# Scaling two units per group inside the FFN products, casting v a group later, and adding part of the product sums on VectorE

## The chip, the cores and the metric

The kernel runs on one core of a Trainium2 chip. A core has TensorE (PE) for matmuls, VectorE (DVE), ScalarE (ACT) and GpSimd (POOL) for elementwise work, and SyncE (SP), which here issues nearly all transfers between memory and the core. Each engine works through its own queue in order; an instruction that must wait holds everything behind it on that queue. The metric is the device time of one execution in microseconds (us), as the median of several runs.

## The reference

Linear attention with a decay per head, and then a feed-forward network (FFN) with a product of two linear maps:

```
for b in range(nb):                       # blocks of the sequence, with a running state
    intra = (qb @ kb.T) * Dmask           # Dmask[i, j] = lam ** (i - j) for i >= j
    out[:, :, sl] = intra @ vb + (qb * lam_pow) @ kv_state
    kv_state = lam_block * kv_state + (kb * rev_pow).T @ vb
...
a = x @ w_a                               # x: the attention's output, 3072 x 512
b = x @ w_b                               # w_a, w_b: 512 x 1536
return (a * b) @ w_out                    # w_out: 1536 x 512
```

q, k and v have 4 batches, 8 heads, 768 positions and 64 dimensions in f32; the result is 3072 x 512 in f32.

## The kernel before

The 3072 rows are cut into 24 *units* of 128 positions, six to a batch. The units are worked on in eight groups of 4, 1, 2, 4, 4, 4, 4 and 1 units (`GROUPS`). While the FFN of group g runs, the attention of the next group's units is prepared in its gaps. So units 0 to 3 are group 0, unit 4 is group 1, 5 and 6 are group 2, 7 to 10 group 3, 11 to 14 group 4, 15 to 18 group 5, 19 to 22 group 6 and 23 group 7.

The order of all work is written out by hand: the program's order is the order on each engine. An FFN calls `hook(slot)` at numbered slots, and the table `PLAN` says, for each group, which piece of work goes at which slot:

- `PK` (`prep_k`): q and k of a unit are multiplied by powers of the decay and become bf16 (two `scale` instructions on POOL, line 283, tile `qk`); then SP issues a transposing DMA of the result (line 313, tile `qkT`).
- `PV` (`prep_v`): v of a unit is cast to bf16 (line 300, on ACT from unit 9 on; tile `vb`), and `pump` is called. `P` is `PK` and `PV` together.
- `S`: the scores of a unit (`kq`, line 341, PE) and their masks (`m`, line 358, DVE).
- `V` (`piece_V`): the unit's part of the state, added into the PSUM bank `kvd` (line 405, PE), and a masked copy of that bank (`st`, line 438, DVE). The last unit of a batch (5, 11, 17, 23) has nothing to do here.
- `Q` and `O2` (`pieces_O`): the attention output of two units (`o_ps`, line 375), its cast into the FFN's input `xT` (line 398, ACT), the state's part of the second unit (line 427) and its copy (line 438). `Q` also makes the scores and masks of the two units that follow.
- `TW` (`w_sums`): sums and differences of weight pieces for the FFN with seven products (tile `tw`, line 515, DVE).
- `W`: one of the seven output rows held back in SBUF from the early groups is stored.

`pump` issues loads in the order of the list `pending`. A load of q, k or v of unit c goes out when c is less than `used` plus two (three up to unit 8), where `used` is the number of units already scaled. All loads, the transposes and the stores of finished rows share SP's queue.

Groups 3 to 6 use `ffn_seven`: the two linear maps are worked out with seven block products instead of eight, for six pairs of column blocks i. A product is four matmuls of 256 columns into a PSUM bank (`m_q`, `m_r`, `m_p`, line 544). Between the products, ACT copies banks to SBUF (line 559: `s1`, `s5`, `s2`, `u2`) and DVE adds (lines 586, `c12`; 592, `c22`; 595, the product with `m_q`). Product 2 goes into `m_p`; ACT copies it, and POOL adds it to the copy of product 1:

```
                snap("s2", p, 0, d["s12"][:, 1])
                bank["held"].discard(pb)
                d["c11"] = a_pool.tile([128, 2, 256], BF16, name="c11", tag="a")
                nc.gpsimd.tensor_add(d["c11"], d["s12"][:, 0], d["s12"][:, 1])
```

POOL then multiplies `c11` and `c12` into the FFN's inner tile `ab` (line 588). The products follow each other in this order, one per step s, for all i: `((0, 1), (2, 5), (3, 2), (4, 6), (6, 3), (8, 7), (12, 4))` gives offset from 7i and number of the product. Slot 2j lies at s = 7j + 1 and slot 2j + 1 at s = 7j + 4, up to slot 10. Slot 11 follows the last step but one. Then come the output matmuls (`op`, line 647), six at a time: slots 12 to 19 lie between these half rows, and a finished row of 128 x 512 is copied by ACT (`o_sb`, line 642) and stored by SP (line 643).

Of the kernel before, what the change touches and what calls it, by code (L numbers as in the profile page):

```python
# [17 lines left out]
BF16 = mybir.dt.bfloat16  # L18
# [4 lines left out]
def _bc(ap, dims):  # L23
# [7 lines left out]
W_HALVES = (4, 5)  # L31
W_BUFS = 11
LOOKAHEAD = {9: 2, 10: 1}
DMA_T = range(7, 24)
KEEP_GROUPS = 3
PACK = 4
# [4 lines left out]


S_GROUPS = (3, 4, 5, 6)
PLAN = {
# [11 lines left out]
}  # L56
for _g, _u in ((3, 11), (4, 15), (5, 19)):
    PLAN.setdefault(_g, []).extend(
        [(11, "PK", _u + 4), (11, "V", _u), (12, "PK", _u + 5), (12, "PV", _u + 4), (13, "Q", (_u, _u + 1, _u + 2, _u + 3)),
         (15, "V", _u + 2), (17, "O2", (_u + 2, _u + 3)), (18, "S", _u + 4)])  # L60
    if _u + 5 > 23:
        PLAN[_g].remove((12, "PK", 24))
    else:
        PLAN[_g] += [(14, "PV", _u + 5), (16, "P", _u + 6), (18, "P", _u + 7), (19, "S", _u + 5)]
PLAN[3] += [(1, "PK", 13), (3, "PK", 14), (8, "PV", 13), (11, "PV", 14)]
PLAN[3] += [(_s, "W", None) for _s in (9, 9, 9, 10, 10, 10, 10)]
PLAN[0] += [(7, "TW", (0, "dve")), (7, "TW", (1, "dve")), ]
PLAN[2] += [(_s, "TW", (4 + _n // 4, "dve", (_n % 4,)))
            for _n, _s in enumerate((2, 3, 5, 6, 8, 15, 15, 15))]


@with_exitstack
def kernel(
# [11 lines left out]
    nc = tc.nc  # L85
    B, H, S, D = q.shape
# [5 lines left out]
    NU = B * NB  # L92
# [12 lines left out]
    a_pool = ctx.enter_context(tc.tile_pool(name="a", bufs=5))  # L105
# [28 lines left out]
    def load_x(w, u):  # L134
        b, nb = divmod(u, NB)
        t = ld_pool.tile([128, H, D], F32, name=w + "f", tag=w + "f", bufs=4 if w == "v" else 3)
        nc.sync.dma_start(out=t, in_={"q": qr, "k": kr, "v": vr}[w][b, nb])  # L137
        raw[u, w] = t
# [16 lines left out]
    def load_w(kind, c):  # L155
        t = wst_pool.tile([128, 1024], F32, name="wst", tag="wst")
        if kind == "o":
            t = t[:].rearrange("p (k n) -> p k n", k=2)
            nc.sync.dma_start(out=t, in_=wo_r[:, 2 * c:2 * c + 2, :])
        else:  # L160
            w = W_CHUNKS[c]
            t = t[:, :KS * w].rearrange("p (k n) -> p k n", k=KS)
            r = wa_r if kind == "a" else wb_r
            if c in W_HALVES:
                t = t.rearrange("p k n -> p (k n)").rearrange("p (k n) -> p k n", k=2)
            nc.sync.dma_start(out=t, in_=w_part(r, c))
        staged[kind, c] = t
# [17 lines left out]
    pending = []  # L185
# [3 lines left out]
    pending += [("o", c) for c in range(4)] + [("q", n0), ("k", n0)]  # L189
    pending += [("o", 4), ("o", 5), ("v", n0)]  # L190
    for u in range(n0 + 1, NU):
        pending += [("q", u), ("k", u), ("v", u)]
    used = {"u": 0}

    def pump():
        while pending:
            kind, c = pending[0]
            if kind in "abo":
                if len(staged) >= W_BUFS:
                    return  # L200
            elif c >= used["u"] + LOOKAHEAD.get(used["u"], 2 if used["u"] > 8 else 3):
                return
            pending.pop(0)
            if kind in "abo":
                load_w(kind, c)
            else:
                load_x(kind, c)
# [26 lines left out]
    for u in range(n0):  # L234
        load_x("v", u)
    pump()


# [66 lines left out]
    def prep_k(u):  # L305
        make_ks(u, "dve" if u < n0 + 2 else "pool")
        make_qs(u, "pool")
        used["u"] = u + 1
        if u in (13, 14):
            pump()  # L310
        if u in DMA_T:
            qkT = qkT_pool.tile([128, 2, HP, 128], BF16, name="qkT", tag="qkT")
            nc.sync.dma_start_transpose(  # L313
                out=qkT[:].rearrange("p j hp i -> p (j hp) i"),
                in_=U[u]["qk"][:].rearrange("p j h d -> p (j h d)"))
            U[u]["qT"], U[u]["kT"] = qkT[:, 0], qkT[:, 1]

    def prep_v(u):
        make_vb(u, "pool" if u < n0 + 3 else "dve" if u < n0 + 5 else "act")
# [197 lines left out]
    def sums(u):  # L517
        g = next(i for i in range(len(GROUPS)) if g_u0[i] <= u < g_u0[i] + GROUPS[i])
        if g not in S_GROUPS or u != g_u0[g] + 3:
            return  # L520
# [11 lines left out]
    def ffn_seven(g, u0, xT, hook):  # L532
# [23 lines left out]
        def snap(name, ps, bufs, t=None):  # L556
            if t is None:
                t = sn_pool.tile([128, 2, 256], F32, name=name, tag=name, bufs=bufs)
            nc.scalar.copy(t, ps)  # L559
            return t  # L560

        def step(i, n):
            d = live.setdefault(i, {})
            if n == 1:
                d["q"], d["qb"] = bank_of("m_q")
                product(i, d["q"], w_of(wa_sb, 0, i), x11, True)
                d["s12"] = wst_pool.tile([128, 2, 2, 256], F32, name="s12", tag="wst")
                snap("s1", d["q"], 0, d["s12"][:, 0])
            elif n == 5:
                d["r"], d["rb"] = bank_of("m_r")  # L570
                product(i, d["r"], t_of(0, i), st[:, 0], True)
                d["s5"] = snap("s5", d["r"], 2)
            elif n == 2:
                p, pb = bank_of("m_p")
                product(i, p, w_of(wa_sb, 2, i), x12, True)
                snap("s2", p, 0, d["s12"][:, 1])
                bank["held"].discard(pb)
                d["c11"] = a_pool.tile([128, 2, 256], BF16, name="c11", tag="a")
                nc.gpsimd.tensor_add(d["c11"], d["s12"][:, 0], d["s12"][:, 1])  # L579
            elif n == 6:  # L580
                product(i, d["q"], t_of(1, i), st[:, 1], False)
                d["u2"] = snap("u2", d["q"], 1)
            elif n == 3:
                product(i, d["r"], w_of(wb_sb, 2, i), st[:, 3], False)
                c12 = sn_pool.tile([128, 2, 256], F32, name="c12", tag="c12", bufs=2)
                nc.vector.tensor_add(c12, d["u2"], d["r"])  # L586
                bank["held"].discard(d["rb"])
                nc.gpsimd.tensor_mul(ab[:, 2 * i:2 * i + 2, 0:256], d["c11"], c12)  # L588
            elif n == 7:
                product(i, d["q"], t_of(2, i), st[:, 2], False)  # L590
                d["c22"] = sn_pool.tile([128, 2, 256], F32, name="c22", tag="c22", bufs=1)
                nc.vector.tensor_add(d["c22"], d["s5"], d["q"])
            else:
                product(i, d["q"], t_of(3, i), x22, False)
                nc.vector.tensor_mul(ab[:, 2 * i:2 * i + 2, 256:512], d["c22"], d["q"])  # L595
                bank["held"].discard(d["qb"])
                live.pop(i)
# [239 lines left out]
    for g, n in enumerate(GROUPS):  # L837
# [33 lines left out]

        if g in S_GROUPS:
            ffn_seven(g, g_u0[g], gx.pop(g), hook)
# [31 lines left out]
```

## Time and profile before

| | before |
|---|---|
| median of 3 runs | 233.31 us (233.29 to 234.09) |
| the profiled execution's time | 231.28 us |
| its span, first to last instruction | 229.6 us |
| mean granted clock of TensorE | 0.993 |
| busy: PE, DVE, ACT, POOL | 217.9, 143.6, 120.8, 110.4 us |
| bytes moved | 39.40 MB |

The profiled execution is one single execution; its rows give start and duration in us from the start of the span. On a row of a timeline, the brackets at the end tell how long the engine had stood idle just before, and which instruction ended that idle time. A row may stand for several like instructions (x4); its duration is then that of all of them. Matmuls overlap, so that of two rows the difference of their starts is the pace, not the duration shown. In a row of windows stand the stretch, its length, the busy time of PE, weight loads, DVE, ACT and POOL, the granted clock as a share of full speed, the share of the DMA engines and the GB/s.

### The profile page before, as it was taken

The numbers are of one execution on the slowest core, as the hardware profiler recorded it, in microseconds if no ns is written. First come the engines' busy times: TensorE is split into PE (matmuls) and PEld (weight loads), VectorE is DVE, ScalarE is ACT, GpSimd is POOL, SyncE is SP. The second block draws the span as 40 slices with busy tenths as digits, with TensorE's granted clock in tenths as the row PEclk, the third lists the DMA queues.
The fourth block names the chain that finished last, engine by engine and source line by source line (L and its number), as shares of the span: only waits on it lengthen the run. The fifth ranks groups of instructions, "written<-read, shape, count | busy, mean of one in ns | idle before, by whom it ended". The sixth has DMA issues, their size and how long they took to land.

```text
span 229.6 us, 5404 instructions
## 1 busy us (share of the span) xinstructions
PE 217.9 (95%) x2127; PEld 149.6 (65%) x2127; DVE 143.6 (63%) x252; ACT 120.8 (53%) x237; POOL 110.4 (48%) x115
## 2 busy tenths in 40 slices
PE   7799999999999997999989999968999999999994
PEld 2475444459688576885548885436886558885494
DVE  0994888986489597669175667039665645663050
ACT  3686564056555565773347663147664337771251
POOL 6061000237455469998338778064878006773000
PEclk9999999999999999999999999997999999999999
DMA  4999999999999999996999902999200421001211
GB/s 134 314 259 353 361 387 302 292 219 198 214 215 171 221 194 222 179 303 203 223 234 234 177 3 49 157 254 251 72 0 3 109 79 46 1 3 46 87 52 46
DMA packets 97544, 39.40 MB, mean 172 GB/s; under 512 B 85488, under 2 KB 92016, under 8 KB 97520
## 3 DMA queue, kind: packets, MB, share of 16 engines
q1 hardware_dynamic: 97232, 39.00, 75.8%
q8 instruction: 16, 0.26, 0.5%
q10 hardware_dynamic: 288, 0.07, 0.1%
q14 instruction: 8, 0.07, 0.1%
HBM read 28.32 MB, written 6.29 MB: 151 GB/s over the span
## 4 chain that ended last, share of the span: by engine, by line
PE 71%; DMA 13%; SPq 5%; DVE 4%; ACT 2%; POOL 2%; issue 1%; ACTq 0%; POOLq 0%
PE op L647 19%; PE m_q L544 17%; PE b_ps L478 9%; PE m_r L544 8%; PE a_ps L478 8%; PE m_p L544 5%; DMA vf<-in_v_dram 4%; DMA out_dram<-o_sb 4%; DMA wst<-in_moe_w_b_dram 3%; SPq L137 3%; PE o_ps L375 3%; DMA q<-in_q_dram 2%; PE kq L341 2%; POOL qk L283 2%; SPq L313 1%
## 5 line engine op out<-in xcount | busy, mean ns | idle before, releaser
L647 PE MATMUL op<-wo_sb,ab 128*128 128x512 bf16 (+2 forms) x312 | 67.3, 363 | 0.0
L647 PEld LDWEIGHTS <-ab 128*128 128x128 bf16 x312 | 28.0, 98 | 27.3
L544 PEld LDWEIGHTS <-tw 128*128 128x128 bf16 x384 | 37.7, 98 | 8.6 <-issue 2.3
L579 POOL TENSOR_TENSOR c<-s 128x512 bf16<-128x512 f32 x24 | 30.6, 1274 | 21.9 <-ACT s L559 21.8
L283 POOL TENSOR_TENSOR qk<-kf,lp_k 128x512 bf16<-128x512 f32 x18 | 19.0, 1054 | 28.8 <-DMA kf<-in_k_dram 25.9
L283 POOL TENSOR_TENSOR qk<-qf,lp_q 128x512 bf16<-128x512 f32 x20 | 21.8, 1091 | 22.7 <-DMA qf<-in_q_dram 22.7
L505 DVE TENSOR_TENSOR ab<-a_sb,b_ps 128x128 bf16<-128x128 bf16 (+2 forms) x48 | 19.3, 417 | 21.4 <-ACT a_sb L487 18.5
L588 POOL TENSOR_TENSOR ab<-c,c 128x512 bf16<-128x512 bf16 x24 | 28.0, 1165 | 6.6 <-DVE c L586 6.2
L595 DVE TENSOR_TENSOR ab<-c,m_q 128x512 bf16<-128x512 f32 x24 | 16.5, 688 | 22.0 <-PE m_q L544 22.0
L358 DVE TENSOR_TENSOR m<-kq,lotri 128x512 bf16<-128x512 f32 x45 | 28.0, 682 | 2.0 <-PE kq L341 1.9
L544 PE MATMUL m_q<-xs,tw 128*128 128x256 bf16 x192 | 29.2, 275 | 0.0
L478 PE MATMUL b_ps<-xT,wb_sb 128*128 128x128 bf16 (+2 forms) x192 | 27.7, 272 | 0.3 <-DVE wb_sb L182 0.3
L478 PE MATMUL a_ps<-xT,wa_sb 128*128 128x128 bf16 (+2 forms) x200 | 27.7, 268 | 0.1
L642 ACT COPY o_sb<-op 128x512 f32<-128x512 f32 (+2 forms) x19 | 10.3, 541 | 31.9 <-PE op L647 29.2
L544 PEld LDWEIGHTS <-wa_sb 128*128 128x128 bf16 x192 | 18.9, 99 | 5.9 <-issue 2.9
L487 ACT CAST a_sb<-a_ps 128x128 bf16<-128x128 f32 (+2 forms) x48 | 17.1, 376 | 10.4 <-PE a_ps L478 9.5
L559 ACT COPY s<-m_q 128x512 f32<-128x512 f32 x24 | 14.1, 587 | 12.5 <-PE m_q L544 11.6
L478 PEld LDWEIGHTS <-wa_sb 128*128 128x128 bf16 x200 | 16.1, 98 | 6.6 <-DVE wa_sb L182 0.3
L478 PEld LDWEIGHTS <-wb_sb 128*128 128x128 bf16 x192 | 15.7, 98 | 6.5 <-DVE wb_sb L182 0.8
L586 DVE TENSOR_TENSOR c<-u,m_r 128x512 f32<-128x512 f32 x24 | 16.3, 680 | 3.2 <-ACT u L559 3.2
L544 PE MATMUL m_p<-xT,wa_sb 128*128 128x256 bf16 x96 | 14.8, 278 | 2.5 <-ACT o_sb L642 2.5
L300 ACT CAST vb<-vf 128x512 bf16<-128x512 f32 x15 | 9.3, 627 | 14.7 <-DMA vf<-in_v_dram 13.6
(85 smaller groups left out, 301.3 us busy)
## 6 DMA issues: line engine op xcount, KB each, us to landing
vf<-in_v_dram SPq DMA_DIRECT2D x24, 256.0 KB, 4.8
qf<-in_q_dram SPq DMA_DIRECT2D x20, 256.0 KB, 4.5
kf<-in_k_dram SPq DMA_DIRECT2D x20, 256.0 KB, 4.8
out_dram<-o_sb SPq DMA_DIRECT2D x16, 256.0 KB, 3.4
wst<-in_moe_w_a_dram SPq DMA_DIRECT2D x6, 512.0 KB, 8.4
wst<-in_moe_w_b_dram SPq DMA_DIRECT2D x6, 512.0 KB, 8.8
wst<-in_moe_w_out_dram SPq DMA_DIRECT2D x6, 512.0 KB, 10.6
out_dram<-o_kept SPq DMA_DIRECT2D x7, 256.0 KB, 3.7
```

Source lines behind the costliest of these rows:

```text
L283: eng_of(eng).tensor_mul(dst.rearrange("p (c b) d -> p b c d", b=2), x[:].rearrange("p (b c) d -> p b c d", b=2), lp.rearrange("p (b c) o ...
L358: nc.vector.tensor_mul(m, kq[i], lotri_bc)
L478: nc.tensor.matmul(ps[:, lo:hi], lhsT=w_sb[:, s, f * 128:(f + 1) * 128], rhs=xT[:, s, lo:hi], start=(s == 0), stop=(s == KS - 1), skip_gro ...
L487: nc.scalar.copy(a_sb[:, :gt], ps[:, :gt])
L505: nc.vector.tensor_mul(ab[:, f, :gt], a_sb[:, :gt], ps[:, :gt])
L544: nc.tensor.matmul(ps[:, f, :], lhsT=w(k, f), rhs=x[:, k, :], start=(first and f == 0 and k == 0), stop=True, skip_group_check=True)
L559: nc.scalar.copy(t, ps)
L579: nc.gpsimd.tensor_add(d["c11"], d["s12"][:, 0], d["s12"][:, 1])
L586: nc.vector.tensor_add(c12, d["u2"], d["r"])
L588: nc.gpsimd.tensor_mul(ab[:, 2 * i:2 * i + 2, 0:256], d["c11"], c12)
L595: nc.vector.tensor_mul(ab[:, 2 * i:2 * i + 2, 256:512], d["c22"], d["q"])
L647: nc.tensor.matmul(op[:, lo:hi], lhsT=ab[:, f, t * 128:(t + 1) * 128], rhs=wo_sb[:, f, lo:hi], start=(f == 0), stop=(f == FC - 1))
```

## The change

- From unit 15 on (`V_LATE`), v is put two units later in the list of loads, and goes out only once its own unit has been scaled; `prep_k` calls `pump` behind the transpose for these units.
- `PK` of unit 15 moves from slot 11 to slot 7 of group 3; 16, 17 and 18 go to slots 12, 14 and 17. In group 4, `PK` of 19 and 20 moves to slots 6 and 9, among the products, 21 and 22 to slots 13 and 16; `PK` of 23 to slot 6 of group 5. Before, four units of a group were scaled at slots 11, 12, 16 and 18.
- `PV` of units 15 to 18 moves from the end of group 3 to slots 1, 3, 5 and 8 of group 4, `PV` of 19 to 22 likewise to group 5, and of 23 to slot 1 of group 6.
- In groups 3, 4 and 5, `V` of the third unit moves from slot 15 to 14, and the second `O2` from slot 17 to 16.
- For the i listed in `SUM_ON_VEC`, DVE adds product 2 straight from PSUM into `c11`; ACT's copy `s2` and POOL's addition are left out. These are 4, 3, 3 and 4 of the six i in groups 3, 4, 5 and 6.
- The last eight pieces of weight sums, before at slots 2, 3, 5, 6, 8 and three times 15 of group 2, go to slots 10, 10 and 12 of group 1 and 2, 3, 5, 6 and 12 of group 2.

```diff
+V_LATE = 15
+SUM_ON_VEC = {3: (1, 2, 3, 4), 4: (2, 3, 4), 5: (2, 3, 4), 6: (1, 2, 3, 4)}
...
-    3: [(11, "S", 11), (11, "S", 12)],
-    6: [(13, "O", 23)],
+    3: [(1, "PK", 13), (3, "PK", 14), (8, "PV", 13), (11, "PV", 14), (11, "S", 11), (11, "S", 12),
+        (7, "PK", 15), (12, "PK", 16), (14, "PK", 17), (17, "PK", 18)],
+    4: [(6, "PK", 19), (9, "PK", 20), (13, "PK", 21), (16, "PK", 22)],
+    5: [(6, "PK", 23)],
+    6: [(1, "PV", 23), (13, "O", 23)],
 }
 for _g, _u in ((3, 11), (4, 15), (5, 19)):
-    PLAN.setdefault(_g, []).extend(
-        [(11, "PK", _u + 4), (11, "V", _u), (12, "PK", _u + 5), (12, "PV", _u + 4), (13, "Q", (_u, _u + 1, _u + 2, _u + 3)),
-         (15, "V", _u + 2), (17, "O2", (_u + 2, _u + 3)), (18, "S", _u + 4)])
-    if _u + 5 > 23:
-        PLAN[_g].remove((12, "PK", 24))
-    else:
-        PLAN[_g] += [(14, "PV", _u + 5), (16, "P", _u + 6), (18, "P", _u + 7), (19, "S", _u + 5)]
-PLAN[3] += [(1, "PK", 13), (3, "PK", 14), (8, "PV", 13), (11, "PV", 14)]
+    PLAN[_g] += [(11, "V", _u), (13, "Q", (_u, _u + 1, _u + 2, _u + 3)), (14, "V", _u + 2),
+                 (16, "O2", (_u + 2, _u + 3)), (18, "S", _u + 4)]
+    if _g < 5:
+        PLAN[_g] += [(19, "S", _u + 5)]
+    if _g > 3:
+        PLAN[_g] += [(1, "PV", _u), (3, "PV", _u + 1), (5, "PV", _u + 2), (8, "PV", _u + 3)]
...
+PLAN[1] += [(10, "TW", (4, "dve", (0,))), (10, "TW", (4, "dve", (1,))), (12, "TW", (4, "dve", (2,)))]
 PLAN[2] += [(_s, "TW", (4 + _n // 4, "dve", (_n % 4,)))
-            for _n, _s in enumerate((2, 3, 5, 6, 8, 15, 15, 15))]
+            for _n, _s in enumerate((2, 3, 5, 6, 12), 3)]
...
-        pending += [("q", u), ("k", u), ("v", u)]
+        pending += [("q", u), ("k", u)]
+        if u < V_LATE:
+            pending += [("v", u)]
+        elif u >= V_LATE + 2:
+            pending += [("v", u - 2)]
+    pending += [("v", NU - 2), ("v", NU - 1)]
...
+            elif kind == "v" and c >= V_LATE:
+                if c >= used["u"]:
+                    return
...
+        late = u >= V_LATE
         if u in DMA_T:
...
+        if late:
+            pump()
...
-                snap("s2", p, 0, d["s12"][:, 1])
+                d["c11"] = a_pool.tile([128, 2, 256], BF16, name="c11", tag="a")
+                if i in SUM_ON_VEC[g]:
+                    nc.vector.tensor_add(d["c11"], d["s12"][:, 0], p)
+                else:
+                    snap("s2", p, 0, d["s12"][:, 1])
+                    nc.gpsimd.tensor_add(d["c11"], d["s12"][:, 0], d["s12"][:, 1])
                 bank["held"].discard(pb)
-                d["c11"] = a_pool.tile([128, 2, 256], BF16, name="c11", tag="a")
-                nc.gpsimd.tensor_add(d["c11"], d["s12"][:, 0], d["s12"][:, 1])
```

## The prediction

> **What bounds the kernel now.** I read four things in this order: the busy shares and the chain on the profile's page, TensorE's timeline for its idle pieces, the timelines of the engines that those pieces name, and the windows for the granted clock.
>
> ```profile
> PE 217.9 (95%) x2127; PEld 149.6 (65%) x2127; DVE 143.6 (63%) x252; ACT 120.8 (53%) x237; POOL 110.4 (48%) x115
> ...
> PE   7799999999999997999989999968999999999994
> ...
> PE 71%; DMA 13%; SPq 5%; DVE 4%; ACT 2%; POOL 2%; issue 1%; ACTq 0%; POOLq 0%
> ```
>
> TensorE (PE) is busy 95% of a span of 229.6 us and carries 71% of the chain; no other engine passes 63%. So only time in which TensorE stands still, or runs slowly, can be won. The 40 slices of 5.74 us show three weak spots inside the run: slice 15 (a 7), slice 20 (an 8) and slices 26 and 27 (6 and 8). They are the starts of groups 3, 4 and 5. TensorE's timeline gives their idle pieces, and two windows the clock:
>
> ```profile
> 88.56 0.60 PE L544 MATMUL m_q<-xT,tw 128*128 128x256 bf16 x4 [1.61 <-DVE c L592]
> ...
> 119.52 0.60 PE L544 MATMUL m_p<-xT,wa_sb 128*128 128x256 bf16 x4 [0.94 <-ACT o_sb L642]
> ...
> 152.17 0.38 PE L341 MATMUL kq<-qkT 64*128 64x128 bf16 x7 [0.75 <-ACT o_sb L642]
> ...
> 153.61 0.60 PE L544 MATMUL m_r<-xs,tw 128*128 128x256 bf16 x4 [0.35 <-DVE xs L524]
> 155.80 1.01 PE L544 MATMUL m_p<-xT,wa_sb 128*128 128x256 bf16 x4 [1.59 <-ACT o_sb L642]
> ...
> 158.80 0.60 PE L544 MATMUL m_q<-xs,tw 128*128 128x256 bf16 x4
> ...
> 152.60:155.80 3.20, 1.20 (x9) 0.77 (x9) 2.63 (x3) 1.76 (x5) 2.23 (x2) 0.87 1.20 294
> 155.80:158.80 3.00, 3.00 (x17) 2.16 (x16) 3.00 (x7) 2.09 (x4) 1.26 (x1) 0.56 1.26 231
> ```
>
> Idle at the three starts: 1.61; 0.94; 0.75 + 0.35 + 1.59 = 2.69 us; together 5.24 us. Besides, the granted clock (the column after the five engines) falls to 0.56 behind the last of them: from 155.80 to 158.80 only four products run, 3.00 us. In the steady state a product takes 0.437 us (below), four of them 1.75, so the slow clock costs 1.25 us.
>
> Why ScalarE (ACT) is late at the starts of groups 4 and 5:
>
> ```profile
> 118.15 0.62 ACT L300 CAST vb<-vf 128x512 bf16<-128x512 f32 x1 [2.77 <-DMA vf<-in_v_dram]
> ...
> 151.02 0.62 ACT L300 CAST vb<-vf 128x512 bf16<-128x512 f32 x1 [5.88 <-DMA vf<-in_v_dram]
> ...
> 154.43 0.62 ACT L300 CAST vb<-vf 128x512 bf16<-128x512 f32 x1 [1.33 <-DMA vf<-in_v_dram]
> 155.16 0.59 ACT L642 COPY o_sb<-op 128x512 f32<-128x512 f32 x1
> ...
> 188.99 0.59 ACT L642 COPY o_sb<-op 128x512 f32<-128x512 f32 x1 [2.45 <-issue]
> 189.61 0.60 PE L544 MATMUL m_p<-xT,wa_sb 128*128 128x256 bf16 x4
> 149.86 1.04 POOL L283 TENSOR_TENSOR qk<-kf,lp_k 128x512 bf16<-128x512 f32 x1 [7.18 <-DMA kf<-in_k_dram]
> 140.70 4.23 SPq L313 DMA_TRANSPOSE qkT<-qk  x2
> 149.49 1.14 SPq L137 DMA_DIRECT2D vf<-in_v_dram  x1
> ```
>
> ACT's queue is in order. A cast of v waits for its load with the copies of the finished output rows (`o_sb`) behind it, and those copies free the PSUM banks that TensorE wants next. The loads are late because SP's queue is in order too: it stands at two transposes until GpSimd (POOL) has scaled units 19 and 20 at the end of the group, and issues a v only at 149.49. The start of group 6 has no such cast: the copy runs at 188.99 and m_p at 189.61 has no idle mark. That is what a start costs without the waits: nothing.
>
> Group 3's start is another matter: VectorE (DVE) still makes the last weight sums.
>
> ```profile
> 84.06 0.60 PE L544 MATMUL m_r<-xs,wb_sb 128*128 128x256 bf16 x4
> ...
> 84.64 1.48 DVE L515 TENSOR_TENSOR tw<-wb_sb 128x512 bf16<-128x512 bf16 x1
> 86.05 1.26 DVE L515 TENSOR_TENSOR tw<-wa_sb,tw 128x512 bf16<-128x512 bf16 x1
> ...
> 87.83 0.67 DVE L592 TENSOR_TENSOR c<-s,m_q 128x512 f32<-128x512 f32 x1
> ```
>
> The sum that m_q waits for is done at 88.50, behind 2.6 us of weight sums; TensorE would have gone on at 88.56 - 1.61 = 86.95.
>
> **The change, part by part.** *Weight sums sooner.* The three sums of slot 15 in group 2 go (two shown). What is late next is m_r's product (84.06 + 0.60) with two sums of 0.67 behind it, done near 86.1, before 86.95: -1.61 us. The sums move to slots 10 and 12 of group 1 and earlier in group 2.
>
> ```profile
> L515 DVE TENSOR_TENSOR tw<-wb_sb,wa_sb x6: 411/418/1283, 33.3 to 71.5; 128x512 bf16<-128x512 bf16 x6
> 59.80 0.28 DVE L505 TENSOR_TENSOR ab<-a_sb,b_ps 128x128 bf16<-128x128 bf16 x1
> 61.01 1.47 PE L647 MATMUL op<-wo_sb,ab 128*128 128x512 bf16 x6
> ```
>
> In group 1 two of them stand before that product at 59.80; at 1.28 (the slowest of this form) and 0.42 it ends at 61.8 at the latest. TensorE reads it in the last of six matmuls that start at 61.01, about 62.1. Cost nothing, with 0.3 us of cover; if that went, what is beyond it.
>
> *v two units later, cast in the next group; units 15 to 23 scaled inside the products.* At the ends of groups 3 and 4 all v casts, and half the scalings, are gone, and no v load is waited for there: -0.94 - 2.69 us, and -1.25 for the clock that falls behind them. The casts move into the products, `PV` at slots 1, 3, 5, 8. There a cast costs ACT 0.62 us, and the cover is ACT's idle time:
>
> ```profile
> 124.78 0.59 ACT L559 COPY s<-m_q 128x512 f32<-128x512 f32 x1 [0.68 <-PE m_q L544]
> ...
> 122.34 0.60 PE L544 MATMUL m_p<-xT,wa_sb 128*128 128x256 bf16 x4
> ...
> 125.40 0.60 PE L544 MATMUL m_p<-xT,wa_sb 128*128 128x256 bf16 x4
> ...
> 125.16 0.69 DVE L592 TENSOR_TENSOR c<-s,m_q 128x512 f32<-128x512 f32 x1
> 126.91 0.69 DVE L595 TENSOR_TENSOR ab<-c,m_q 128x512 bf16<-128x512 f32 x1 [1.06 <-PE m_q L544]
> DMA to landing us min/median/max: 4.4/4.8/6.9
> ```
>
> A step of seven products takes 125.40 - 122.34 = 3.06 us (0.437 each). ACT idles at least 0.68 in it, and 0.59 more wherever a snapshot goes: 0. But behind each cast now stand the snapshots on which TensorE's accumulation waits, so a late v would stall the products. The shortest lead is v of unit 18: issued behind the transpose of slot 17, so before group 4's first product, and cast at slot 8, 29 products later, 29 x 0.437 = 12.7 us. A v lands in 6.9 us at most, so some 6 us are spare. On SP each transpose moves with its scaling, and with it the two or three loads behind it; what stands behind those is output stores, for which ACT waits only three rows later. The transpose of unit 21 must also wait until group 4's slot 13 has read unit 15's buffer, a microsecond with loads for the next group behind it: 0.
>
> *Product sums on VectorE.* In 14 of 24 steps a snapshot (ACT) and an add (POOL) go, and VectorE adds from PSUM.
>
> ```profile
> L592 DVE TENSOR_TENSOR c<-s,m_q 128x512 f32<-128x512 f32 x24 | 16.4, 685 | 0.4
> ...
> L579 POOL TENSOR_TENSOR c<-s 128x512 bf16<-128x512 f32 x24 | 30.6, 1274 | 21.9 <-ACT s L559 21.8
> ```
>
> The add has L592's operands (one f32 from SBUF, one from PSUM), so I take 0.69 us; 1.48, the slowest two-input row here, is the other end. VectorE idles 1.06 us in a step (row 126.91), just where the add falls: cost 0 at 0.69, and 14 x (1.48 - 1.06) = 5.9 us at the far end. POOL loses 1.27 us in each such step, 14 x 1.27 = 17.8 us, and takes in units 15, 19, 20 and 23, twice 1.04 us each (row 149.86 is one of the two), 8.3: it stays inside the steps.
>
> *Slots moved up at the end of a group* (V from 15 to 14, O2 from 17 to 16). O2 earlier only adds lead. V does not: its matmuls add into the bank that VectorE is still reading.
>
> ```profile
> 107.53 2.75 PE L647 MATMUL op<-wo_sb,ab 128*128 128x512 bf16 x12
> 110.12 0.39 PE L405 MATMUL kvd<-vb,qk 128*128 128x128 bf16 x4
> ...
> 108.77 0.68 DVE L438 TENSOR_TENSOR st<-kvd,bdiag 128x512 bf16<-128x512 f32 x1
> ...
> 179.15 2.76 PE L647 MATMUL op<-wo_sb,ab 128*128 128x512 bf16 x12
> ...
> 180.40 0.68 DVE L438 TENSOR_TENSOR st<-kvd,bdiag 128x512 bf16<-128x512 f32 x1
> ```
>
> In group 3 V 13 now comes after six of the twelve matmuls, 107.53 + 1.30 = 108.83, but the state copy, queued behind four masks, ends at 109.45; with 0.06 us from VectorE's end to TensorE's start (88.50 to 88.56 above) that is a new wait of 0.68. Group 5, V 21: 180.45 against 181.14, 0.69. In group 4 unit 17 ends a sequence and V does nothing. Together +1.37; the bounds are 0 and twice that.
>
> *The sum.* The profiled execution took 231.28 us (1.68 around its span). 231.28 - 1.61 - 0.94 - 2.69 - 1.25 + 1.37 = 226.16. The median of the runs, 233.31, lies 2.03 above that execution; I carry this over: **228.2 us**.
>
> *A rule weighed.* The row is 152.60:155.80: busy 1.20 of 3.20 us, no single idle piece over 1.59, and the clock fell; behind 1.61 us of idle in group 3 it did not. The Trainium skill, "TensorE: Matmul & The Clock Gate" (Why this matters for your kernels), warns only of idle gaps over some 3 us. By that the clock's fall has another cause and the 1.25 us may stay: 229.4. The trace speaks against that reading, and for the same page's Part 1, by which a free-running window of about 3.4 us of activity decides.
>
> **The rivals.**
> 1. *More is won.* The 2.03 us between the median and the profiled execution may be slow clock too: each of the three starts holds idle that another run can find in a worse place, at 1.25 us each. With the idle gone it goes: 226.2. For it: the fall at 155.8. Against: three runs within 0.8 us of each other. (The Trainium skill's free-running window, same page, Part 1, would allow it; no run here shows it.)
> 2. *VectorE becomes the bound.* At 1.27 us (what POOL needs for this add; near the slow weight sum, 1.26) an add passes the cover by 0.21 us; 14 x 0.21 = 2.9: 231.1. Against: L592 averaged 685 ns over 24 runs, with POOL's L579 in the same steps.
> 3. *The waits go only in part.* Another late transfer or bank holds a start: half of the 3.63 + 1.25 us of groups 4 and 5 stays, 2.4: 230.6. If all of it stays, which is the change not doing what it says, 228.2 + 4.9 = 233.1, no difference. Against: group 6's start without idle.
> 4. *The clock falls anyway* (the rule above, taken as the whole truth): 229.4.
> 5. *Slower: casts late inside the products.* ACT's waits for v were 1.33 to 5.88 us above. From two late casts at 2.77 (5.5 us) on, the gain is gone; with three (units 16 to 18), 3 x 2.77 = 8.3: 236.5. For it: SP's queue has stood for POOL. Against: the 6 us spare.
>
> **How the numbers follow.** Forecast 0.54 (own range 227.0 to 229.4: half the offset, or twice the V wait); rival 1, 0.12; rival 2, 0.09; rival 3 in part 0.10 and in full 0.06; rival 4, 0.05; rival 5, 0.04. The range reaches from 225.4 (rival 1, and no V wait) to 231.6 (rivals 2 and 3 with a little more), and leaves out rival 5, rival 3 in full and the tails. Half a per cent, 1.17 us, is about what a measurement can tell from no change: faster means under 232.1. Forecast and rivals 1, 2, 4 and most of 3 are faster, 0.88; 0.07 the same; 0.05 slower.
>
> **What would show it.** Right: TensorE's timeline without idle marks at the starts of groups 3, 4 and 5, the granted clock 1.00 there, casts of v without DMA waits; two new marks of about 0.7 at kvd in groups 3 and 5; the add 14 times at 0.69 on VectorE, POOL's add 10 times. Wrong: idle marks inside the seven products (m_q, m_r waiting for an ACT snapshot behind a cast, or for VectorE), or steps longer than 3.06 us.

## The result, and the profile after

The changed kernel takes 225.38 us (median of 4 runs, 224.93 to 226.04) against 233.42 (4 runs, 233.29 to 234.09): a ratio of 0.9652, 95% interval 0.9621 to 0.9684. It is faster, as forecast, but by 8.0 us instead of 5.1. Its profiled execution took 225.55 us, against the 226.16 of the prediction's sum: that sum was 0.6 off, and the 2.03 us added to it for the median did not come. (The ratios here leave out runs more than 1.5% above the fastest run of their kernel; medians and spreads in this text are of all runs.)

The profile's page of the changed kernel: the busy shares, PE's 40 slices with the granted clock, and the chain by engine.

```profile
PE 216.9 (97%) x2127; PEld 149.4 (67%) x2127; DVE 150.9 (67%) x266; ACT 114.7 (51%) x223; POOL 92.1 (41%) x101
...
PE   7899999999999999999999999999999999999994
...
PEclk9999999999999999999999999999999999999999
...
PE 74%; DMA 12%; DVE 6%; SPq 4%; ACT 1%; issue 1%; ACTq 0%; DVEq 0%
```

The weak slices 15, 20, 26 and 27 are nines now, the clock is full throughout, and POOL has left the chain. TensorE's timeline at the starts of groups 3 (86.71, 87.15), 4 (117.68) and 5 (150.55), and at the two places where the new wait for the state copy was forecast (108.10, 174.73, each with the output matmuls ahead of it):

```profile
86.71 0.60 PE L559 MATMUL m_q<-xs,tw 128*128 128x256 bf16 x4
87.15 0.60 PE L559 MATMUL m_q<-xT,tw 128*128 128x256 bf16 x4
...
106.12 1.46 PE L665 MATMUL op<-wo_sb,ab 128*128 128x512 bf16 x6
...
108.10 0.38 PE L420 MATMUL kvd<-vb,qk 128*128 128x128 bf16 x4 [0.52 <-DVE st L453]
...
117.68 0.60 PE L559 MATMUL m_p<-xT,wa_sb 128*128 128x256 bf16 x4
...
150.55 0.60 PE L559 MATMUL m_p<-xT,wa_sb 128*128 128x256 bf16 x4
...
172.76 1.47 PE L665 MATMUL op<-wo_sb,ab 128*128 128x512 bf16 x6
...
174.73 0.38 PE L420 MATMUL kvd<-vb,qk 128*128 128x128 bf16 x4 [0.51 <-DVE st L453]
```

No product has an idle mark any more; the only new ones are the two at `kvd`.

Matmuls of equal size give a second measure, the pace. The distance from the first product of one group to that of the next holds everything that happened between them. In us (start of group 3, then the lengths of groups 3 to 6; group 7's first matmul ends the last):

| | start of 3 | group 3 | group 4 | group 5 | group 6 |
|---|---|---|---|---|---|
| before | 82.24 | 35.29 | 35.13 | 36.08 | 29.67 |
| after | 82.61 | 34.19 | 32.87 | 33.34 | 29.67 |
| difference | +0.37 | -1.10 | -2.26 | -2.74 | 0.00 |

The sum is -5.73, which is 225.55 - 231.28. So the difference of these two profiled executions lies in the three places that were forecast. The rest of the 8.0 us is not in these two executions, but in what other executions of the kernel before do; a second profile of it (e9) has other lengths.

### The profile page after: what moved, and what is told of

Its sections match the earlier page's. It is cut to its first block, busy times and chain, and to the rows that moved or that the text cites. A ratio compares the mean times of both kernels' runs of the same rounds, so it can differ in the third digit from the quotient of the medians.

```text
span 223.8 us, 5380 instructions
## 1 busy us (share of the span) xinstructions
PE 216.9 (97%) x2127; PEld 149.4 (67%) x2127; DVE 150.9 (67%) x266; ACT 114.7 (51%) x223; POOL 92.1 (41%) x101
## 4 chain that ended last, share of the span: by engine, by line
PE 74%; DMA 12%; DVE 6%; SPq 4%; ACT 1%; issue 1%; ACTq 0%; DVEq 0%
PE op L665 23%; PE m_q L559 19%; PE m_r L559 9%; DMA wst<-in_moe_w_b_dram 8%; PE b_ps L493 5%; PE a_ps L493 5%; PE m_p L559 5%; PE o_ps L390 3%; DVE m L373 3%; SPq L141 2%; PE kq L356 2%; DMA q<-in_q_dram 2%; DMA wst<-in_moe_w_out_dram 2%; DVE tw L530 2%; PE kvd L420 1%; SPq L163 1%
## 5 line engine op out<-in xcount | busy, mean ns | idle before, releaser
L596 POOL TENSOR_TENSOR c<-s 128x512 bf16<-128x512 f32 x10 | 12.7, 1274 | 30.1 <-ACT s L574 30.1
L413 ACT CAST xT<-o_ps 128x512 bf16<-128x512 f32 (+1 forms) x24 | 12.2, 553 | 9.7 <-PE o_ps L390 9.5
L610 DVE TENSOR_TENSOR c<-s,m_q 128x512 f32<-128x512 f32 x24 | 16.4, 685 | 0.4
```

## The experiments

The lengths of groups 3 to 6 of the profiled executions, in us:

| | 3 | 4 | 5 | 6 |
|---|---|---|---|---|
| e1, weight sums alone | 33.52 | 38.11 | 36.08 | 29.67 |
| e2, products repeated | 34.82 | 35.62 | 36.07 | 29.67 |
| e3, V back to slot 15 | 33.51 | 33.08 | 32.67 | 29.67 |
| e4, no sums on VectorE | 36.19 | 34.10 | 33.34 | 29.66 |
| e5, v cast at the end | 34.20 | 33.40 | 33.34 | 29.67 |
| e6, scaling at the end | 34.19 | 32.90 | 35.46 | 29.67 |
| e7, sums on VectorE alone | 33.96 | 38.79 | 36.36 | 29.67 |
| e8, state copied first | 33.51 | 32.87 | 32.67 | 29.67 |
| e9, before again | 34.30 | 38.68 | 36.26 | 29.67 |

**e1: the kernel before, with only the weight sums sooner.**

```diff
+PLAN[1] += [(10, "TW", (4, "dve", (0,))), (10, "TW", (4, "dve", (1,))), (12, "TW", (4, "dve", (2,)))]
-            for _n, _s in enumerate((2, 3, 5, 6, 8, 15, 15, 15))]
+            for _n, _s in enumerate((2, 3, 5, 6, 12), 3)]
```

> The kernel before with one part of the change: the weight sums at their new slots of groups 1 and 2. Theory A (the change's parts pay for themselves one by one, at the pace of the products): only group 3's stop goes, 2.22 us from product to product less 0.44 = 1.78 us, so 231.6 from 233.4. Theory B (idle marks are the price): 1.61, 231.8. Theory C (the kernel before loses more to slow clock in its usual runs than in its profiled one, and group 3's idle is one of the places): up to 1.25 us more, 230.4. If the sums in group 1 cost something: above 231.8.

Measured: 233.72 us (232.14 to 235.45, 12 runs), before 232.94; ratio 1.0081, interval 1.0041 to 1.0121. Group 3 gains the 1.77 us in full, and group 4 loses 2.98. TensorE's and ACT's timelines of e1:

```profile
120.58 0.60 PE L545 MATMUL m_p<-xT,wa_sb 128*128 128x256 bf16 x4 [3.09 <-ACT o_sb L643]
...
117.85 0.62 ACT L301 CAST vb<-vf 128x512 bf16<-128x512 f32 x1 [2.52 <-DMA vf<-in_v_dram]
119.94 0.58 ACT L643 COPY o_sb<-op 128x512 f32<-128x512 f32 x1 [1.47 <-DMA out_dram<-o_sb]
```

The work came to the start of group 4 1.09 us earlier than in the first profile of the kernel before, v only 0.30 earlier, and the copy behind it, which waits for the store of an output row, 1.06 later; the stop was 3.09 us instead of 0.94. Since the unchanged kernel can have nearly the same stop (e9: 2.92), this profile alone does not show that the earlier arrival made it. What the 12 runs show is that the prediction's first step gains nothing by itself. Theories A, B and C all missed. The number falls to the last branch, but its reason is not seen: group 3 starts at 82.92, inside the scatter of all executions here (82.1 to 83.6).

**e2: the kernel before, with some bank-opening products repeated, so that TensorE works through its idle pieces.** The repeated products write the same values again. This was to tell slow clock from late work.

```diff
-                product(i, d["r"], t_of(0, i), st[:, 0], True)
+                for _ in range(1 + ({4: 2, 5: 3}.get(g, 0) if i == 0 else 0)):
+                    product(i, d["r"], t_of(0, i), st[:, 0], True)
...
-                product(i, p, w_of(wa_sb, 2, i), x12, True)
+                for _ in range(1 + (3 if (g, i) == (3, 1) else 0)):
+                    product(i, p, w_of(wa_sb, 2, i), x12, True)
```

> The kernel before, with TensorE's idle time at the starts of groups 3, 4 and 5 filled: a product that opens a bank is made three, two and three times more than needed (its last result is the right one), so that TensorE works where it stood idle, and nothing else moves. Theory C (slow clock behind idle time): the granted clock stays 1.00, the profiled time falls by the 1.25 us of slow clock to about 230.0, and the runs' median, if all of its 2.0 us above the profiled time is slow clock too, to about 230.0 as well, 3.4 under 233.4. Theory D (those 2.0 us have another cause): the median falls by 1.25 only, to 232.2. If the clock's fall has nothing to do with idle time: 233.4 and a window of 0.56 as before.

Measured: 232.41 us (231.47 to 233.84, 12 runs); ratio 1.0026, interval 0.9983 to 1.0068. The clock is full in this profile, and 0.998 or more in 11 of the 12 runs. The window of e2 where the kernel before had 0.56:

```profile
155.80:158.80 3.00, 2.46 (x21) 1.86 (x20) 3.00 (x6) 2.29 (x6) 1.57 (x2) 1.00 1.32 237
```

Yet nothing was won there. VectorE's and TensorE's timelines of e2:

```profile
157.28 2.47 DVE L358 TENSOR_TENSOR m<-kq,lotri 128x512 bf16<-128x512 f32 x4
...
160.27 0.67 DVE L594 TENSOR_TENSOR c<-s,m_q 128x512 f32<-128x512 f32 x1
...
160.99 0.60 PE L544 MATMUL m_q<-xT,tw 128*128 128x256 bf16 x4 [0.64 <-DVE c L594]
```

The group's first product is at 153.04, so the one at 160.99 comes 7.95 us later. In the kernel before, at half the clock, the same two are at 152.66 and 160.62, 7.96 apart; its VectorE and TensorE:

```profile
153.59 1.27 DVE L525 TENSOR_TENSOR xs<-xs,xT 128x512 bf16<-128x512 bf16 x1
154.79 1.26 DVE L526 TENSOR_TENSOR xs<-xT 128x512 bf16<-128x512 bf16 x1
...
156.90 2.47 DVE L358 TENSOR_TENSOR m<-kq,lotri 128x512 bf16<-128x512 f32 x4
...
159.89 0.68 DVE L592 TENSOR_TENSOR c<-s,m_q 128x512 f32<-128x512 f32 x1
151.20 0.23 PE L341 MATMUL kq<-qkT 64*128 64x128 bf16 x1
...
152.66 0.60 PE L544 MATMUL m_q<-xT,wa_sb 128*128 128x256 bf16 x4
...
160.62 0.60 PE L544 MATMUL m_q<-xT,tw 128*128 128x256 bf16 x4
```

VectorE's queue (four sums of columns of x, two of them at 1.27, the state copy, four masks of 2.47 together, two sums) decided when that product could start; the slow clock there cost nothing. e1 agrees: at this place its clock stayed at 1.00, and its group 5 is 36.08 long all the same. Neither reading of the offset came out cleanly: the runs drew together (2.4 us from lowest to highest, against 5.7 of the kernel before on that chip), but not to a lower time.

**e3 and e12: the changed kernel, with V back at slot 15 and O2 at 17.**

```diff
-    PLAN[_g] += [... (14, "V", _u + 2), (16, "O2", (_u + 2, _u + 3)), ...]
+    PLAN[_g] += [... (15, "V", _u + 2), (17, "O2", (_u + 2, _u + 3)), ...]
```

> The changed kernel with V of the third unit back at slot 15 and the second O2 back at slot 17 in groups 3, 4 and 5. If the new wait at V costs what the pace shows (1.98 and 1.97 us where 1.30 were, 0.68 and 0.67): 225.4 - 1.35 = 224.0. If it costs what the idle marks show (0.52 and 0.51): 224.4. Rival: the later O2 takes the lead from the next group's start, and a wait of the same size comes there: 225.4 or above.

Measured: 224.66 us (223.83 to 225.43, 6 runs); ratio to before 0.9697, interval 0.9641 to 0.9753. Groups 3 and 5 are shorter by 0.68 and 0.67, which is the forecast price of the wait (0.68 and 0.69); group 4 is longer by 0.21. There, with O2 a slot later, two of VectorE's sums of columns of x run beside POOL's scaling and take 1.15 and 1.26 us instead of 0.42, and a product waits for VectorE's queue (e12: 0.33 longer). The median lies 0.7 below the changed kernel's, between what the lengths give (1.14) and the rival's nothing.

**e4: the changed kernel, all product sums back on ACT and POOL** (`SUM_ON_VEC` empty).

```diff
-SUM_ON_VEC = {3: (1, 2, 3, 4), 4: (2, 3, 4), 5: (2, 3, 4), 6: (1, 2, 3, 4)}
+SUM_ON_VEC = {3: (), 4: (), 5: (), 6: ()}
```

> The changed kernel with all product sums on GpSimd again, behind ScalarE's copy, and all else as changed. If the sums on VectorE are only what makes room for the scalings on GpSimd: GpSimd then has 6 x 2.43 + 2 x 2.08 = 18.7 us of work in the 18.3 us of group 4's products and about 21 in group 3's, so that its last products come 0.5 to 3 us late and TensorE waits once at the first output rows of a group: 226 to 229. If they matter to nothing: 225.4. If VectorE's adds cost the changed kernel time: below 225.2.

Measured: 228.57 us (228.11 to 229.07, 6 runs); ratio 0.9865, interval 0.9811 to 0.9918. Groups 3 and 4 are longer by 2.00 and 1.23. TensorE's and POOL's timelines of e4:

```profile
106.10 0.60 PE L665 MATMUL op<-wo_sb,ab 128*128 128x512 bf16 x2 [1.41 <-POOL ab L606]
...
141.09 0.60 PE L665 MATMUL op<-wo_sb,ab 128*128 128x512 bf16 x2 [1.06 <-POOL ab L606]
...
103.54 1.27 POOL L596 TENSOR_TENSOR c<-s 128x512 bf16<-128x512 f32 x1
104.88 1.16 POOL L606 TENSOR_TENSOR ab<-c,c 128x512 bf16<-128x512 bf16 x1
```

With units scaled among the products, POOL ends its products of the last i too late, and the output matmuls wait for `ab`. The sums on VectorE are what makes room for the scaling; about 3.2 us of the change rest on them.

**e5: the changed kernel, with v loaded and cast in the old places.**

```diff
-V_LATE = 15
+V_LATE = 24
-    6: [(1, "PV", 23), (13, "O", 23)],
+    6: [(13, "O", 23)],
-    if _g > 3:
-        PLAN[_g] += [(1, "PV", _u), (3, "PV", _u + 1), (5, "PV", _u + 2), (8, "PV", _u + 3)]
+    PLAN[_g] += [(_s, "PV", _u + 4 + _n) for _n, _s in enumerate((12, 14, 16, 18)) if _u + 4 + _n < 24]
...
-        late = u >= V_LATE
+        late = u >= 15
```

> The changed kernel with v loaded in the old order (beside q and k of its unit) and cast at the end of the group again (slots 12, 14, 16, 18); q and k are still scaled early, inside the products. Theory P (the stops at the starts of groups 4 and 5 came from scaling late: SP's queue stood at the transposes and every load behind them was late): with early scalings the v loads go out early too, no cast waits, 225.4 as changed. Theory V (v two units later, in the next group, is what is needed): ScalarE waits for v at the group's end, stops of 0.9 to 3 us at each of the two starts: 227 to 231.

Measured: 229.41 us (225.81 to 230.84, 6 runs); ratio 0.9793, interval 0.9715 to 0.9871. The profiled execution happens to be the fastest of the six, and shows how near the edge it runs:

```profile
116.57 0.62 ACT L310 CAST vb<-vf 128x512 bf16<-128x512 f32 x1 [2.70 <-DMA vf<-in_v_dram]
...
117.93 0.60 PE L557 MATMUL m_p<-xT,wa_sb 128*128 128x256 bf16 x4 [0.34 <-ACT o_sb L658]
```

A cast at the end of a group still waits 2.70 us for its load, and in this execution 0.34 us of that reached TensorE. The other five took 1.9 to 5.0 us more; where, no trace shows. The runs fit theory V; the one profile shows its wait, but hardly its cost.

**e6: the changed kernel, with the units scaled in the old places, and v still late.**

```diff
-        (7, "PK", 15), (12, "PK", 16), (14, "PK", 17), (17, "PK", 18)],
-    4: [(6, "PK", 19), (9, "PK", 20), (13, "PK", 21), (16, "PK", 22)],
-    5: [(6, "PK", 23)],
+        (11, "PK", 15), (12, "PK", 16), (16, "PK", 17), (18, "PK", 18)],
+    4: [(11, "PK", 19), (12, "PK", 20), (16, "PK", 21), (18, "PK", 22)],
+    5: [(11, "PK", 23)],
```

> The other half: v late and cast in the next group as changed, but the scalings of units 15 to 23 back at slots 11, 12, 16 and 18. Theory P: the loads of q and k wait again behind transposes that wait for GpSimd, the last scores of a group come late, and TensorE stops 0.5 to 3 us before the starts of groups 4 and 5: 227 to 230. Theory V: ScalarE's queue has no v load to wait for, the copies of the output rows run on time: 225.4.

Measured: 228.32 us (227.2 to 230.02, 6 runs); ratio 0.9835, interval 0.9783 to 0.9888. The timelines of SP, ACT and TensorE ahead of the start of group 5:

```profile
142.87 2.19 SPq L326 DMA_TRANSPOSE qkT<-qk  x1
...
147.25 1.46 SPq L661 DMA_DIRECT2D out_dram<-o_sb  x2
...
151.53 0.59 ACT L660 COPY o_sb<-op 128x512 f32<-128x512 f32 x1 [5.00 <-DMA out_dram<-o_sb]
...
152.17 0.60 PE L559 MATMUL m_p<-xT,wa_sb 128*128 128x256 bf16 x4 [1.92 <-ACT o_sb L660]
```

There is no cast in front of the copy, and TensorE stops all the same: the copy waits 5.00 us for a buffer whose row is not stored yet, because the stores stand on SP behind a transpose and its three loads, and go out at 147.25, two together. In the changed kernel they go out singly, at 139.01, 145.12 and 148.29. The start of group 4 has no stop here. Theory P has the time, but not the path: the stores were late, not the scores. So e6 shows that the early scaling holds off a wait for stores, and e5, less firmly, that the late casts hold off waits for v. With either part taken back, about 3 to 4 us of the 8.0 are lost.

**e7: the kernel before, with only the sums on VectorE** (the last hunk of the change, and the table `SUM_ON_VEC`).

> The kernel before with the product sums on VectorE alone. The stops before the starts of groups 4 and 5 are set by loads, and GpSimd is not what they wait for in the first place: 233, no difference. If GpSimd's work behind the products is what makes its scalings late (in group 4 the first scaling starts right behind its last product): they start up to 1 us earlier, 231 to 232. If VectorE's adds cost: above 233.5.

Measured: 232.13 us (229.69 to 234.66, 12 runs); ratio 0.995, interval 0.9901 to 0.9998. Its profile, of one of its longer runs (234.13), shows the stop at the start of group 4 again, 3.94 us before m_p behind a cast that waited 4.23 us for its v. Its groups 3 and 4 (33.96, 38.79) are close to those of the unchanged kernel in e9 (34.30, 38.68), so this profile does not show where a gain would have gone. By the runs, the sums alone give about 0.5%.

**e8 and e11: the changed kernel, with the state copied between the masks of the two units** instead of behind all four masks.

```diff
-        for u, kq in zip(nxt, kqs):
+        copy = beside and us[1] % NB < NB - 1
+        for n_u, (u, kq) in enumerate(zip(nxt, kqs)):
             masks(u, kq)
-        if beside and us[1] % NB < NB - 1:
+            if copy and n_u == 0:
+                kv_copy(us[1], kv["ps"])
+        if copy and not nxt:
             kv_copy(us[1], kv["ps"])
```

> The changed kernel with the state's copy queued on VectorE between the masks of the two units instead of behind all four: V then finds its bank free at slot 14. The copy ends some 2.4 us after the scores' start, V comes 2.9 us after it: both new waits go, 0.68 + 0.67: 224.0, and the next group's start keeps the lead of the earlier O2. Rival: the second unit's masks, 0.7 us later, hold the output matmuls that read them: 225.4.

Measured: 224.06 us (223.78 to 224.38, 6 runs); ratio 0.9645, interval 0.9601 to 0.9690. The two new waits are gone: TensorE's timeline in group 3, against 106.12 and 108.10 [0.52] above, and VectorE's copy:

```profile
106.31 1.46 PE L668 MATMUL op<-wo_sb,ab 128*128 128x512 bf16 x6
...
107.60 0.39 PE L420 MATMUL kvd<-vb,qk 128*128 128x128 bf16 x4
...
106.51 0.69 DVE L453 TENSOR_TENSOR st<-kvd,bdiag 128x512 bf16<-128x512 f32 x1
```

**e9: the kernel before, profiled once more.** This asked where the median's 2.03 us above the first profiled execution lie.

> The kernel before, unchanged, for a second profile. Theory W (its runs differ by how long ScalarE waits for v loads, and the first profiled execution, 231.28, was one of the shorter ones): the same stops at the starts of groups 3, 4 and 5 with other lengths, runs anywhere between 230 and 236, and the time above or below 231.28 is found in these stops alone. Theory K (a constant 2 us beside the profiled execution): a profile of about 231.3 again and runs at 233.3.

Measured: 235.14 us in the profiled execution, 3.86 more than the first one, and 233.66 in the other run. (Against 11 more runs of the same kernel the ratio is 1.0148, interval 1.0033 to 1.0263; differences of the size of e1's and e7's should be read with that in mind.) Group 4 is 3.55 us longer (38.68 against 35.13). TensorE's and ACT's timelines at its start:

```profile
118.10 0.60 PE L544 MATMUL m_r<-xs,tw 128*128 128x256 bf16 x4
121.62 0.60 PE L544 MATMUL m_p<-xT,wa_sb 128*128 128x256 bf16 x4 [2.92 <-ACT o_sb L642]
...
125.96 0.60 PE L544 MATMUL m_p<-xT,wa_sb 128*128 128x256 bf16 x4
...
119.06 0.62 ACT L300 CAST vb<-vf 128x512 bf16<-128x512 f32 x1 [3.03 <-DMA vf<-in_v_dram]
...
120.98 0.58 ACT L642 COPY o_sb<-op 128x512 f32<-128x512 f32 x1 [1.31 <-DMA out_dram<-o_sb]
```

Two windows of the same execution, the second behind the first:

```profile
118.20:121.60 3.40, 0.50 (x5) 0.29 (x4) 2.48 (x5) 1.23 (x3) 1.63 (x2) 1.00 1.19 167
122.10:125.40 3.30, 3.30 (x18) 2.34 (x16) 0.69 (x1) 2.11 (x4) 1.79 (x2) 0.52 1.36 224
```

The same stop as in the first profile, but 2.92 us instead of 0.94, because v and a store came later; and after 3.40 us with 0.50 us of work the granted clock falls to 0.52 for the next 3.30 us. The start of group 4 is thus where these two executions differ; e1 and e7 have the long stop at the same place. Besides, group 3 starts 1.11 us later here and is 0.99 shorter, which nearly cancel. The rows of the clock on the two pages, the first profile's ahead, have one slice below full at the start of group 5, and in e9 a second one at the start of group 4:

```profile
PEclk9999999999999999999999999997999999999999
...
PEclk9999999999999999999997999997999999999999
```

With one such slice the mean clock is 0.993, with two 0.985. The mean clocks of 51 other runs of the kernel before fit it: medians of 230.5 us at 0.998 to 1.000 (10 runs), 231.8 at 0.993 (13) and 233.7 at 0.985 (18), the others between 233.1 and 236.0 with clocks of 0.978 to 0.992. The first profiled execution is one of 0.993. Against this execution the changed kernel's profile gains 0.1, 5.8 and 2.9 us in groups 3, 4 and 5, not 1.1, 2.3 and 2.7.

**e10, e11 and e12: the changed kernel, the state copied first, and V back, once more on one chip.**

> The changed kernel, beside the next two on one chip. Theory W: no transfer is waited for behind the start, so its runs lie within some 1.2 us, at 225.4.

> The changed kernel with the state's copy between the masks, beside the changed kernel on one chip: 1.35 us less by the pace of the two stops (224.0), 1.0 less by their idle marks (224.4).

> The changed kernel with V at slot 15 and the second O2 at slot 17, beside the changed kernel on one chip: 1.35 us less by the pace of the two stops, 1.0 less by their idle marks; if the earlier O2 carried part of the gain, up to 1 us of that comes back at the starts of the groups.

Measured: 225.54 us (225.05 to 226.43, 6 runs), 224.48 (223.78 to 225.12, 6) and 224.81 (224.22 to 225.69, 6), with ratios to before of 0.9765 (interval 0.9709 to 0.9821), 0.9712 (0.9652 to 0.9772) and 0.9734 (0.9677 to 0.9790). The second profile of the changed kernel has the same lengths of groups (34.19, 32.87, 33.34). The two variants are 1.1 and 0.7 us below it; the intervals overlap, and what carries the difference is the lengths of groups 3 and 5, each 0.66 to 0.68 shorter in both variants, in both profiles of each (with V back, group 4 is 0.2 to 0.3 longer). The version with the state copied first was the fastest of all that ran, below both kernels.

## Why the prediction was right or wrong

**What failed: the last step.** "The median of the runs, 233.31, lies 2.03 above that execution; I carry this over." The forecast of 228.2 is 2.8 too high: 2.0 of it is this step, 0.6 the sum, and 0.2 the median of the changed kernel lying below its own profiled execution. What such an offset is made of, e9 showed in one execution: a longer stop at the start of group 4 and the slow clock behind it. That most executions are of that kind is not shown by a trace, but 28 of the 51 runs have a mean clock below 0.993, which fits. The change takes away the cast that waits there, so the offset goes with it: ten runs of the changed kernel lie within 1.5 us, at clocks of 0.999 to 1.000. That was rival 1 (226.2, with a chance of 0.12). Its argument, that the stops fall in worse places in other executions, is borne out by e9; but the clock is the smaller part there. Of the 3.55 us in group 4, 1.98 are the longer stop by pace (3.08 against 1.10, from the rows of m_r and m_p: 3.52 and 1.54, less 0.437). Of the 1.57 that remain, 1.52 lie between this m_p and the next one (121.62 to 125.96 against 119.52 to 122.34), where the clock is 0.52. "Against: three runs within 0.8 us of each other" was weak evidence: over 51 runs the spread is 6.6 us. That the profiled execution lay 2.0 below all three should have weighed more. The ends of the ranges do not follow from their own words either: 226.16 without the V wait of 1.37 is 224.8, not 225.4, and half the offset below 228.2 is 227.2, not 227.0. The measured 225.38 lies between the first two. TensorE's timeline of the kernel before, for this and the next point:

```profile
86.34 0.60 PE L544 MATMUL m_q<-xs,tw 128*128 128x256 bf16 x4
...
117.98 0.60 PE L544 MATMUL m_r<-xs,tw 128*128 128x256 bf16 x4
```

**Weight sums, -1.61.** Right, and undersized: by the pace 1.78 (86.34 to 88.56 is 2.22, less 0.437), and group 3 shows 1.10 = 1.78 - 0.68. Cost nothing in groups 1 and 2 held within the scatter of group 3's start (82.1 to 83.6 over all executions here). But the size is not fixed: in e9 the last two sums took 0.41 and 1.49 us instead of 1.48 and 1.26, and the stop is marked 0.63 instead of 1.61. And e1 showed that this step gains nothing by itself.

**The ends of groups 3 and 4, -0.94 - 2.69.** Right in place and cause, and undersized in the same way (that half the scalings leave the ends holds for group 4 only; in group 3 it is one of four). A product's row shows 0.60 us, while products follow each other at 0.437: the idle mark counts from the modelled end of the last matmul, and so each stop is some 0.16 us longer than its mark. The stop ahead of `kq` is longer still, because one matmul of the eight had already gone: 1.13 by pace, from the first kq to m_q (151.20 to 152.66 is 1.46, in the changed kernel 0.33):

```profile
149.34 0.40 PE L356 MATMUL kq<-qkT 64*128 64x128 bf16 x8
149.67 0.61 PE L559 MATMUL m_q<-xT,wa_sb 128*128 128x256 bf16 x4
```

So the two stops in group 4 are 1.10 and 1.13, which is all but 0.03 of its 2.26. The five marks of the prediction sum to 5.24, the five stops by pace to 6.27 (1.78, 1.10, 1.13, 0.51 and 1.75). That missing 1.03 is what the sum of the prediction had too little; the start of group 3, later by 0.37, hid part of it.

**The clock, -1.25.** The time was there (from the m_p at 155.80 to the m_q at 160.62 are 4.82 us, in the changed kernel from 150.55 to 154.22 3.67, which is 1.15 less), the reason was wrong. e2 had the full clock at that place and no gain, because VectorE's queue held the product at 160.62. After the change this queue is done earlier: with nothing late in front of it, the four sums of columns of x lie ahead of the group's first product (149.67), and each takes 0.42 us where two took 1.27 and 1.26 beside POOL's scaling. The earlier scaling does this, not the earlier O2: with the scaling back (e6) two of these sums take 1.15 and 1.26 again, with O2 back (e3) all four stay at 0.42. VectorE's timeline of the changed kernel, and the product that waited before:

```profile
146.14 0.42 DVE L540 TENSOR_TENSOR xs<-xs,xT 128x512 bf16<-128x512 bf16 x1
...
146.81 0.42 DVE L542 TENSOR_TENSOR xs<-xT,xs 128x512 bf16<-128x512 bf16 x1
...
154.22 0.60 PE L559 MATMUL m_q<-xT,tw 128*128 128x256 bf16 x4
```

At the start of group 4 in e9, by contrast, VectorE waits for TensorE and the clock of 0.52 costs the 1.52 us worked out above. The rule weighed was that of the Trainium skill, "TensorE: Matmul & The Clock Gate". Its table under "Why this matters for your kernels" warns of idle gaps over some 3 us; here the clock fell behind 2.92 us of idle in one piece, and behind 2.69 in three pieces. Its Part 1, a free-running window of about 3.4 us of activity, agrees with both (0.50 us busy of 3.40, 1.20 of 3.20). But in e1 the start of group 5 is as empty (1.24 of 3.20 from 154.40 on), and the clock stays at 1.00 behind it: a stretch like this one can pass, and what decides it no run here shows. Rival 4 fell all the same: no start is left empty, and the clock is full.

**The new wait at V, +1.37.** Right: 0.68 and 0.67 by pace (106.12 to 108.10 is 1.98, 172.76 to 174.73 is 1.97, where six matmuls take 1.30), and in e3 and e8 the lengths of groups 3 and 5 fall by just this price.

**Casts in the products, 0.** Right: no cast of v from unit 15 on waits for its load, so rival 5 fell. ACT's timeline of the changed kernel at slot 1 of group 4, the cast and the next copy of a product:

```profile
119.41 0.65 ACT L312 CAST vb<-vf 128x512 bf16<-128x512 f32 x1
119.94 0.62 ACT L574 COPY s<-m_q 128x512 f32<-128x512 f32 x1
```

The step "what stands behind those is output stores, for which ACT waits only three rows later" was priced at 0, which holds for the change; but it was a thin cover. In e6 the copy waited 5.00 us for those stores, and TensorE stood 1.92 by its mark. "O2 earlier only adds lead" was priced at nothing too; by e3 and e12 it is worth 0.2 to 0.3 us in group 4.

**Sums on VectorE, 0.** Right: 14 of them at 687 ns against 0.69 taken, and POOL's ten at 1274; rival 2 fell. The groups of the changed kernel:

```profile
L593 DVE TENSOR_TENSOR c<-s,m_p 128x512 bf16<-128x512 f32 x14 | 9.6, 687 | 3.6 <-PE m_p L559 3.6
...
L596 POOL TENSOR_TENSOR c<-s 128x512 bf16<-128x512 f32 x10 | 12.7, 1274 | 30.1 <-ACT s L574 30.1
```

The prediction set the 17.8 us that POOL loses against the 8.3 that it takes in; e4 puts the price on it: without the sums on VectorE the scaling among the products costs 3.2 us.

Rival 3 (a part of the waits stays) fell too: no product at any start has an idle mark. What stays open is where the slower runs of e5 lost their time, and how the stops of the kernel before are spread over its other executions, of which two were profiled.

## What to carry to other kernels

When the one profiled execution differs from the median of the runs, the difference is itself made of work at some place; before carrying it over, ask whether it lies in the waits that the change removes. Parts of a schedule that share a boundary are not worth the sum of their separate gains: here two of the parts alone moved the time by less than 1% (ratios of 1.0081 and 0.995). The likely reason, which no run here isolates, is that work which comes early to the next boundary only waits longer there for the same transfer. Price a stop by the distance between equal instructions, not by its idle mark, and before charging a slow clock, look whether another engine's queue would have held the next product anyway.

## What the runs showed of the hardware

- The idle marks of TensorE understate a stop between products by about 0.16 us (0.60 shown for a product, 0.437 its pace), and the stop inside `kq` by 0.38 (0.75 marked, 1.13 by pace).
- A granted clock of 0.56 for 3.00 us cost nothing in one place (by e2 and e1) and one of 0.52 for 3.30 us about 1.5 us in another (e9).
- VectorE's bf16 sum of two SBUF tiles took 1.26 us beside POOL's scaling and 0.42 without. In the profiles of before, after and e9 every sum of this form that took over 0.5 us overlaps an instruction of POOL.
- How long a transfer keeps waiting engines differs from execution to execution: the cast at the start of group 4 waited 2.77 and 3.03 us in two profiles of the same kernel, the copy behind it 0 and 1.31. The kernel before spread over 6.6 us in 51 runs, the changed one over 1.5 in 10.
